# One attention and mixer block on one core: narrow matmuls gathered in two of a group's six slots

## The chip, the core and the metric

The kernel runs on one core of one Trainium2 chip. The core has five engines with a queue of instructions each: PE (TensorE, matmuls), DVE (VectorE), ACT (ScalarE), POOL (GpSimd) and SP (here it issues the DMAs). The metric is the device time of one execution in microseconds; lower is better.

## The reference

Three stages follow one another on inputs of 2 batches, 8 heads, 768 positions and head size 64 (a model width of 512):

```
q_assign = argmax(q_n @ c_n)          # 16 centroids per head
k_assign = argmax(k_n @ c_n)
mask = q_assign[:, None] == k_assign[None, :]
scores = where(mask, scale * q @ k.T, -1e9)
attn = exp(scores - max) / sum        # rows
x = attn @ v                          # -> [2, 768, 512]
...
theta = x @ w_theta
y = w_tok_r @ (x * cos(theta)) + w_tok_i @ (x * sin(theta))
u = x + y;  x = u + relu(u @ w_ch)
...
u = x + V.T @ (U.T @ x)
out = u + relu(u @ w_ch1) @ w_ch2
```

The change touches the first stage alone, the masked attention.

## The kernel before

A *group* is one batch with two of its heads; there are eight (NG = 8, the loop variable `g`). A head's 768 positions are six tiles of 128. The function `attention` runs the groups one after the other, and each group is written out as six *slots* `p` = 0 to 5. The order of the code is the order of every engine's queue; nothing reorders it later. One slot holds

- `scores_pair(g, h, a)`: the scores of two key tiles of one head (8 matmuls, tile `st`, line 303; wide, with 128 rows of output), which ACT turns into exponentials (tile `p`, line 308, four instructions on three banks);
- `max_pair(g + 1, ...)`: scores of the next group for its row maxima (4 matmuls, tile `smax`, line 251; wide), which DVE reduces from three banks (tile `mx`, line 255); after slots 2 and 5 `max_join` puts a head's maxima together (lines 260, 270, 271).

Besides there are the *narrow* matmuls, which write 32 rows of output or fewer:

- `pv`, the value products (line 316): twelve steps a group, taken from the queue `pvq` by `next_pv`; the code puts up to four into each of slots 1, 3 and 5. After the last, ACT copies the result to `xT` (line 323);
- `sum_keys`, the row sums of one half of the keys (tile `l`, line 335), which DVE transposes (tile `lt`, line 338); `row_sums` then takes the reciprocals (lines 343, 345);
- `max_rows`, the maxima as rows (tile `mrow`, line 281), copied by ACT;
- `sims`, the similarities with the centroids (line 121), the first of the items of `assign_items(g)`. DVE transposes them (tile `s_t`, line 124), and the items after it (lines 128 to 152, DVE) make the one-hot assignments that `mask_rows` needs.

Work without a fixed place stands in the queue `bg`: splitting q and k of group g + 2 and packing them by DMA, the assignments, `spread` and `norm_x` (lines 357 and 361, DVE). `fill(t)` takes items off it until their listed costs come to `t`; when `bg` is empty it takes steps of the conversion of the later weights (lines 388, 392 and 396 on DVE, one weight tile in three steps; 384 and 401 on ACT, 405 on POOL). Each slot ends with `fill(1.8)`.

PSUM has eight banks, handed out in turn: `bank()` takes the first of the list `ring` and puts it at the end again. From the first `pv` step of a group to its last, two of them are kept out of the ring. A slot takes three banks for `st` and three for `smax`.

`prologue` prepares groups 0 and 1 and also runs all items of `assign_items(2)`, ahead of `mask_direct(1, 0)` of slot 0 (line 181), whose result the first `smax` matmul of that slot needs. After the attention, `mixer` does the other two stages.

Of the kernel before, what the change touches and what calls it, by code (L numbers as in the profile page):

```python
# [24 lines left out]
NG = B * NP  # L25
# [16 lines left out]
def tile_cluster_block(ctx: ExitStack, tc: tile.TileContext, qk, v, cent, wth, wr, wi, wch,  # L42
# [24 lines left out]
    def give(keep):  # L67
        ring.extend(kept.pop(keep))
# [43 lines left out]
    def cols(hf):  # L112
        return slice(hf * HALF, (hf + 1) * HALF)
# [214 lines left out]
    def sum_keys(g, a):  # L328

        ps = bank("l")  # L330
        for kt in range(3 * a, 3 * a + 3):
            for h in range(2):
                for hf in range(2):
                    o = 32 * (2 * h + hf)
                    nc.tensor.matmul(out=ps[o:o + 32, :HALF], lhsT=ones, rhs=pt[g, h, kt][:, cols(hf)],  # L335
                                     start=(kt == 3 * a), stop=(kt == 3 * a + 2))
        lt = slot("lt")[:, :HALF]
        nc.vector.transpose(lt, ps[:, :HALF])
        lsum[g, a] = lt
# [330 lines left out]


    bg = deque()

    owed = [0.]

    def fill(t):

        owed[0] += t
        while owed[0] > 0:
            if bg:  # L680
                c, f = bg.popleft()
                f()
                owed[0] -= c
            else:
                conv_step()
                owed[0] -= 1.
# [7 lines left out]
    def attention():  # L694


        ORDER = [(0, 0), (0, 2), (0, 4), (1, 0), (1, 2), (1, 4)]
        pvq = deque()
        held[0] = True

        def next_pv():
            g, kt, hf = pvq.popleft()
            pv(g, kt, hf)
            if kt == NT - 1 and hf:
                pv_out(g)

        for g in range(NG):
            nxt = g + 1 < NG
            if nxt:
                load_v(g + 1)  # L710
            if g + 2 < NG:
                bg.extend(split_items(g + 2, nc.gpsimd))
                if g > 0:
                    bg.extend(assign_items(g + 2))
            if g + 3 < NG:
                for i in range(2):
                    load_raw(g + 3, i)
            if g == 1:
                conv_load.extend(weigh_in(wth, NP * DM, wth_t))
                conv_start()  # L720
            if g == 2:
                tok = [c for p in zip(weigh_in(wr, NT * S, wr_t), weigh_in(wi, NT * S, wi_t)) for c in p]
                conv_load.extend(tok[:6])
                conv_start()
                late = tok[6:]
            if g == 6:
                conv_load.extend(late)
                conv_start()
            if not nxt:
                for t in range(NP):  # L730
                    bg.append((0, lambda t=t: split_x(0, t, nc.gpsimd)))
            order = [(1, 0), None, (1, 2), None, (1, 4), None] if g == 0 else ORDER
            for p in range(NT):
                ready = len(pvq)
                if order[p]:
                    h, a = order[p]
                    scores_pair(g, h, a)
                    if h:
                        pvq.extend((g, kt, hf) for kt in (a, a + 1) for hf in range(2))
                if g == 0 and p < 2:  # L740
                    mask_direct(1, p, nc.scalar if p else nc.vector)
                if nxt:
                    max_pair(g + 1, p // 3, 2 * p % 6)
                    if p % 3 == 2:
                        max_join(g + 1, p // 3)

                while conv_after:
                    conv_after.popleft()()
                if p == 3 and g + 2 < NG:
                    mask_rows(g + 2)  # L750
                if g > 0 and p == 1:
                    sum_keys(g - 1, 1)
                if p == 5:
                    sum_keys(g, 0)
                if p % 2:
                    for _ in range(min(ready, 4)):
                        next_pv()
                if g > 0 and p == 1:
                    row_sums(g - 1)
                if g > 0 and p == 5:  # L760
                    bg.appendleft((.95, lambda: norm_x(g - 1)))
                    bg.appendleft((.97, lambda: spread(g - 1)))
                fill(1.8 if nxt else 2.)
                if g > 0 and p == 1:
                    max_rows(g, 1)
                if nxt and p == 3:
                    max_rows(g + 1, 0)
            while bg:
                fill(.5)
        held[0] = False  # L770
        while len(pvq) > 1:
            next_pv()
        nc.scalar.activation(out=warm, in_=warm, func=AF.Sin)
        next_pv()
        sum_keys(NG - 1, 1)

    def prologue():
        hot = slot("hot", BF16)
        nc.vector.memset(hot[:, :512], 0.0)
        hp = bank("hot", "hot")  # L780

        def heat(n):

            for _ in range(n):
                nc.tensor.matmul(out=hp, lhsT=hot[:, :P], rhs=hot[:, :512], start=True, stop=True)

        nc.sync.dma_start(out=cst_sb, in_=cst)
        nc.sync.dma_start(out=cent_sb, in_=cent)
        for g in range(2):
            for i in range(2):  # L790
                load_raw(g, i)
        nc.vector.memset(warm, 1.0)
        nc.scalar.activation(out=warm, in_=warm, func=AF.Sqrt)
        nc.vector.memset(ones, 1.0)
        nc.vector.memset(cblk, 0.0)
        for j in range(2):
            nc.vector.memset(kmul[64 * j:64 * j + 64, 0:1], BIG if j else 1.0)
            nc.vector.memset(kmul[64 * j:64 * j + 64, 1:2], -BIG if j else 0.0)
        nc.vector.memset(kmul[:, 2:3], -BIG)
        nc.vector.memset(halfpi, TWO_PI / 4)  # L800
        init_packs(0, nc.gpsimd)
        heat(9)

        nc.vector.tensor_tensor(csq, cent_sb, cent_sb, op=ALU.mult)
        nc.vector.tensor_reduce(cn2[:, 0:1], csq, axis=AX.X, op=ALU.add)
        nc.scalar.activation(out=cn2[:, 1:2], in_=cn2[:, 0:1], func=AF.Sqrt)
        nc.scalar.activation(out=warm, in_=warm, func=AF.Exp)
        nc.vector.tensor_scalar_add(cn2[:, 1:2], cn2[:, 1:2], 1e-6)
        nc.vector.reciprocal(cn2[:, 2:3], cn2[:, 1:2])
        for j in range(2):  # L810
            nc.vector.tensor_scalar(cdup[:, j], cent_sb, cn2[:, 2:3], None, op0=ALU.mult)
        nc.vector.tensor_copy(cvals, cst_sb[:, 128:160])
        nc.vector.tensor_copy(identb, ident)
        ct = bank("ct")
        nc.tensor.transpose(ct[:, :P], cdup.rearrange("p a d -> p (a d)"), ident)
        cv = ct[:, :P].rearrange("p (a h c) -> p a h c", a=NP, h=2)
        nc.vector.tensor_copy(cblk[0:64, :, 0:16], cv[0:64, :, 0])
        nc.vector.tensor_copy(cblk[64:128, :, 16:32], cv[64:128, :, 1])

        def run(items):  # L820
            for it in items:
                it[1]()

        its, its1 = assign_items(0), assign_items(1)
        for i in range(2):
            split_hi(0, i)
        split_lo(0, 0, nc.gpsimd)
        run(its[:1])
        pack_direct(0, 0)
        pack_direct(0, 1)  # L830
        pack(0, main=())
        load_v(0)
        for i in range(2):
            load_raw(2, i)

        init_packs(1, nc.gpsimd)
        heat(14)
        run(its[1:])
        run(its1[:1])
        mask_direct(0, 0, nc.vector)  # L840
        mask_direct(0, 1, nc.scalar)
        split_lo(0, 1, nc.gpsimd)
        pack_low(0, (0, 1))
        for i in range(2):
            split_hi(1, i)
            split_lo(1, i, nc.gpsimd)
        pack_direct(1, 0)
        pack(1, main=(1,))
        pack_low(1, (0,))
        for a in (0, 2, 4):  # L850
            max_pair(0, 0, a)
        max_join(0, 0, act=True)
        max_pair(0, 1, 0)
        max_pair(0, 1, 2)
        max_rows(0, 0)
        init_packs(2, nc.gpsimd)
        scores_pair(0, 0, 0)
        max_pair(0, 1, 4)
        max_join(0, 1)
        run(its1[1:])  # L860
        scores_pair(0, 0, 2)
        heat(2)
        scores_pair(0, 0, 4)
        heat(2)
        max_rows(0, 1)
        run(assign_items(2))
        give("hot")

    def mixer():
# [136 lines left out]
```

## Time and profile before

| | us |
|---|---|
| three runs, median (lowest to highest) | 702.51 (698.29 to 702.58) |
| the profiled execution, its own time | 700.68 |
| its span, first to last instruction | 698.9 |
| PE busy in the span | 684.9 |
| DVE busy in the span | 456.6 |
| ACT busy in the span | 303.3 |

The span is what the trace covers; the 1.8 us between it and the execution's own time lie around the program. The attention runs from about 31 us to about 240 us of the span. PE's busy share counts pipelined matmuls whose ends are modelled, so how fast it goes is read from the starts of successive rows.

### The profile page before, as it was taken

What the parts mean: (1) busy time and instruction counts of PE and PEld (TensorE: products, weight loads), DVE (VectorE), ACT (ScalarE), POOL (GpSimd) and SP (SyncE); (2) the same over time, 40 slices, a digit from 0 to 9 for tenths busy, and PEclk for the clock granted to TensorE, in tenths of its full rate; (3) what the DMA queues carried; (4) which work ended last, traced back from release to release, by engine and by line L of the source; (5) the groups of instructions that cost most, each with busy time, mean ns of one, the idle gap of its engine ahead of it and who ended that gap; (6) DMA issues with size and microseconds to landing.
All of it is one profiled execution on the core that took longest, in us unless ns stands there. A gap on an engine that the chain in (4) does not pass through costs nothing.

```text
span 698.9 us, 11387 instructions
## 1 busy us (share of the span) xinstructions
PE 684.9 (98%) x4492; PEld 545.7 (78%) x4492; DVE 456.6 (65%) x752; ACT 303.3 (43%) x617; POOL 186.3 (27%) x186
## 2 busy tenths in 40 slices
PE   7799999999999999999999999999999999999997
PEld 3456566565565599999999998888888889888986
DVE  6967987987989476568684985565555656432222
ACT  8636566665677555554555442322222222211110
POOL 9413323323238432114244120222121212100000
PEclk9899999999999999999999999999999999999999
DMA  6779667766322211013220220112122120000112
GB/s 213 189 158 295 199 157 191 218 162 137 126 91 90 92 40 38 1 31 106 80 66 3 90 91 1 46 46 90 51 86 77 59 76 30 1 1 0 61 47 74
DMA packets 21109, 63.11 MB, mean 90 GB/s; under 512 B 4192, under 2 KB 6112, under 8 KB 21056
## 3 DMA queue, kind: packets, MB, share of 16 engines
q1 hardware_dynamic: 21056, 62.39, 30.1%
q8 instruction: 35, 0.57, 0.3%
q14 instruction: 18, 0.15, 0.1%
HBM read 40.94 MB, written 3.15 MB: 63 GB/s over the span
## 4 chain that ended last, share of the span: by engine, by line
PE 89%; DVE 6%; ACT 2%; issue 1%; DMA 1%; POOL 1%; SPq 0%; DVEq 0%; POOLq 0%
PE g L634 19%; PE acc L654 19%; PE y L520 14%; PE st L303 8%; PE pv L316 8%; PE h L538 5%; PE th L478 5%; PE l L335 4%; PE smax L251 4%; DVE mx L255 2%; PE h L589 2%; DVE cv L396 1%; PE th L482 1%; PE sims L121 1%; DMA raw<-in_qk_dram 1%
## 5 line engine op out<-in xcount | busy, mean ns | idle before, releaser
L405 POOL TENSOR_TENSOR wl<-cv,wh 128x768 fp32r<-128x768 f32 (+1 forms) x40 | 78.3, 1959 | 232.6 <-ACT wh L401 175.3
L641 DVE SCALAR_TENSOR_TENSOR gl<-g,gh 128x512 fp32r<-128x512 f32 x48 | 33.1, 690 | 133.1 <-ACT gh L639 133.1
L639 ACT ACTIVATE gh<-g 128x512 fp32r<-128x512 f32 x48 | 28.7, 599 | 206.2 <-PE g L634 206.2
L255 DVE TENSOR_REDUCE mx<-smax 128x1 f32<-128x512 f32 x144 | 90.0, 683 | 24.3 <-PE smax L251 24.0
L308 ACT ACTIVATE p<-st 128x512 f32<-128x512 f32 x192 | 79.2, 506 | 26.6 <-PE st L303 26.1
L520 PE MATMUL y<-wh,z 128*128 128x384 f32 x384 | 87.6, 340 | 0.3 <-ACT z L498 0.3
L634 PE MATMUL g<-uh,wh 128*128 128x512 f32 (+1 forms) x256 | 86.9, 340 | 0.0
L634 PE MATMUL g<-uh,wl 128*128 128x512 f32 (+1 forms) x256 | 86.5, 338 | 0.0
L634 PE MATMUL g<-ul,wh 128*128 128x512 f32 (+1 forms) x256 | 86.1, 336 | 0.0
L303 PE MATMUL st<-qp,kp 128*128 128x256 f32 (+1 forms) x384 | 79.9, 351 | 0.8 <-ACT qp L284 0.3
L654 PE MATMUL acc<-gh,wh 128*128 128x512 f32 x192 | 75.9, 395 | 0.0
L654 PE MATMUL acc<-gh,wl 128*128 128x512 f32 x192 | 75.6, 394 | 0.0
L654 PE MATMUL acc<-gl,wh 128*128 128x512 f32 x192 | 75.3, 392 | 0.0
L303 PEld LDWEIGHTS st<-qp,kp 128*128 128x128 f32 x384 | 57.2, 191 | 18.2 <-issue 6.0
L520 PEld LDWEIGHTS y<-wh,z 128*128 128x128 f32 x384 | 66.9, 188 | 0.5 <-ACT z L498 0.5
L316 PE MATMUL pv<-p,v 128*32 128x384 f32 x768 | 66.2, 487 | 0.0
L392 DVE SCALAR_TENSOR_TENSOR cv<-st,cv 128x768 int32<-128x768 int32 (+2 forms) x42 | 64.6, 1537 | 1.0
L634 PEld LDWEIGHTS g<-ul,wh 128*128 128x128 f32 x256 | 48.5, 189 | 6.1
L634 PEld LDWEIGHTS g<-uh,wl 128*128 128x128 f32 x256 | 48.5, 189 | 5.8
L634 PEld LDWEIGHTS g<-uh,wh 128*128 128x128 f32 x256 | 48.4, 189 | 5.7
L316 PEld LDWEIGHTS pv<-p,v 128*32 128x32 f32 x768 | 24.1, 110 | 36.0 <-issue 35.4
L520 PE MATMUL y<-wl,z 128*128 128x384 f32 x192 | 48.8, 335 | 0.0
(128 smaller groups left out, 1172.9 us busy)
## 6 DMA issues: line engine op xcount, KB each, us to landing
st<-in_w_dram SPq DMA_DIRECT2D x20, 768.0 KB, 4.0
raw<-in_qk_dram SPq DMA_DIRECT2D x16, 384.0 KB, 4.9
qp<-hi SPq DMA_DIRECT2D x26, 192.0 KB, 2.9
st<-in_wr_dram SPq DMA_DIRECT2D x6, 768.0 KB, 4.3
st<-in_wi_dram SPq DMA_DIRECT2D x6, 768.0 KB, 4.2
kp<-hi SPq DMA_DIRECT2D x32, 96.0 KB, 3.0
qp<-lo SPq DMA_DIRECT2D x32, 96.0 KB, 2.8
v<-in_v_dram SPq DMA_DIRECT2D x8, 384.0 KB, 4.0
```

Source lines behind the costliest of these rows:

```text
L255: nc.vector.tensor_reduce(mx_t[g, h][:, o:o + n], ps.rearrange("p (n w) -> p n w", n=n), axis=AX.X, op=ALU.max)
L303: nc.tensor.matmul(out=ps[:, c:c + n], lhsT=kp[s, h, w][:, (a + j) * P:(a + j + 1) * P], rhs=qp[s, h, w][:, q0:q0 + n], start=(w == 0), st ...
L308: nc.scalar.activation(out=pt[g, h, a + j][:, q0:q0 + n], in_=ps[:, c:c + n], func=AF.Exp, scale=float(D) ** -0.5)
L316: nc.tensor.matmul(out=pvt[g][hf][r:r + 32, :HALF], lhsT=v_t[g][:, kt, r:r + 32], rhs=pt[g, r // 64, kt][:, cols(hf)], start=(kt == 0), st ...
L392: nc.vector.scalar_tensor_tensor(t, self.hw, SIGN, t, op0=ALU.bitwise_and, op1=ALU.bitwise_or)
L405: nc.gpsimd.tensor_tensor(t[:, :c.w], c.t, f32(c.hi[:, :c.w]), op=ALU.subtract)
L478: nc.tensor.matmul(out=ps[:, 1], lhsT=xs[b, t][a][:, st * P:(st + 1) * P], rhs=wv[c], start=(n == 0), stop=(n == 11))
L520: nc.tensor.matmul(out=yps[u, j][hf][:, :HALF], lhsT=lhs, rhs=w[st][e][:, hf * HALF:(hf + 1) * HALF], start=(st == 0 and n == 0), stop=(st ...
L538: nc.tensor.matmul(out=ps[hf][:, :HALF], lhsT=wv[a], rhs=xs[b, t][c][:, hf * HALF:(hf + 1) * HALF], start=(n == 0), stop=(n == 11))
L634: nc.tensor.matmul(out=ps[:, o:o + w], lhsT=wv[a], rhs=us[b, t][e][:, s0:s0 + w], start=(n == 0), stop=(n == 11))
L641: nc.vector.scalar_tensor_tensor(gl, ps, 0.0, f32(gh), op0=ALU.max, op1=ALU.subtract)
L654: nc.tensor.matmul(out=aps[c, e], lhsT=wv[a], rhs=g[x], start=(first and i == 0), stop=(last and i == 2))
```

## The change

The slots 2 and 5 (`BURST`) now hold all narrow matmuls: rows of maxima, row sums, up to six value-product steps, and in slot 5 also the similarities of group g + 3, one group earlier than before. `fill` gets 4.8 in those two slots and 0.3 in the four others (10.8 a group, as before). The other items of `assign_items(g + 3)` are kept in `assign` and go into `bg` at the start of the next group. In the prologue the last four items of group 2 are kept back in the same way.

```diff
+    assign = {}
...
+        BURST = (2, 5)
...
-                if g > 0:
-                    bg.extend(assign_items(g + 2))
+                bg.extend(assign.pop(g + 2))
...
-                if g > 0 and p == 1:
-                    sum_keys(g - 1, 1)
-                if p == 5:
-                    sum_keys(g, 0)
-                if p % 2:
-                    for _ in range(min(ready, 4)):
+                if p in BURST:
+                    if p == 2 and g > 0:
+                        max_rows(g, 1)
+                        sum_keys(g - 1, 1)
+                    if p == 5:
+                        if nxt:
+                            max_rows(g + 1, 0)
+                        sum_keys(g, 0)
+                    for _ in range(min(ready, 6)):
                         next_pv()
-                if g > 0 and p == 1:
+                    if p == 5 and g + 3 < NG:
+                        (_, sims), *assign[g + 3] = assign_items(g + 3)
+                        sims()
+                if g > 0 and p == 2:
                     row_sums(g - 1)
...
-                fill(1.8 if nxt else 2.)
-                if g > 0 and p == 1:
-                    max_rows(g, 1)
-                if nxt and p == 3:
-                    max_rows(g + 1, 0)
+                fill(2. if not nxt else 4.8 if p in BURST else .3)
...
-        run(assign_items(2))
+        its2 = assign_items(2)
+        run(its2[:4])
+        assign[2] = its2[4:]
```

On PE, at the border from group 1 to group 2, the similarities (`sims`) stood between the row maxima and the scores of slots 0 and 1. Before:

```order
L251 MATMUL smax<-kp_87,qp_85 128x256 x2
L251 MATMUL smax<-kp_87,qp_85 128x512
L121 MATMUL sims<-raw_0_732,cblk 32x384
L121 MATMUL sims<-raw_1_734,cblk 32x384
L121 MATMUL sims<-raw_0_732,cblk 32x384
L121 MATMUL sims<-raw_1_734,cblk 32x384
L303 MATMUL st<-qp_101,kp_103 128x512
L303 MATMUL st<-qp_102,kp_104 128x512
```

Now they stand at the end of slot 5 of group 1, behind the value products:

```order
L316 MATMUL pv<-p_792,v_461 32x384 x2
L316 MATMUL pv<-p_946,v_461 32x384 x2
L121 MATMUL sims<-raw_0_728,cblk 32x384
L121 MATMUL sims<-raw_1_730,cblk 32x384
L121 MATMUL sims<-raw_0_728,cblk 32x384
L121 MATMUL sims<-raw_1_730,cblk 32x384
L303 MATMUL st<-qp_101,kp_103 128x512
L303 MATMUL st<-qp_102,kp_104 128x512
```

They moved from the inside of a wide stretch to the last place of a narrow one.

On DVE, at the same border (from the transpose of the row sums in slot 5 to the reductions of `smax` in slot 0), before:

```order
L338 STREAM_TRANSPOSE lt<-l 128x384
L357 STREAM_TRANSPOSE rb<-rl 128x768
L361 TENSOR_TENSOR xT_727<-xT_727,rb 128x768
L255 TENSOR_REDUCE mx_1084<-smax 128x1
L255 TENSOR_REDUCE mx_1084<-smax 128x2
L255 TENSOR_REDUCE mx_1084<-smax 128x1
L124 STREAM_TRANSPOSE s_t<-sims 128x384
L128 TENSOR_REDUCE mxc<-s_t 128x24
```

Now:

```order
L338 STREAM_TRANSPOSE lt<-l 128x384
L124 STREAM_TRANSPOSE s_t<-sims 128x384
L357 STREAM_TRANSPOSE rb<-rl 128x768
L361 TENSOR_TENSOR xT_883<-xT_883,rb 128x768
L392 SCALAR_TENSOR_TENSOR cv<-st,cv 128x768
L396 SCALAR_TENSOR_TENSOR cv<-st,cv 128x768
L388 TENSOR_SCALAR cv<-cv 128x768
L255 TENSOR_REDUCE mx_1095<-smax 128x1
L255 TENSOR_REDUCE mx_1095<-smax 128x2
```

The transpose of the similarities moved ahead of `spread` and `norm_x`, and three conversion steps now stand ahead of the reductions of slot 0.

On DVE, at the end of the prologue, before:

```order
L128 TENSOR_REDUCE mxc<-s_t 128x24
L132 TENSOR_TENSOR eqw<-s_t,mxc 128x384
L138 TENSOR_TENSOR eqw<-eqw,cvals 128x384
L143 TENSOR_REDUCE mi<-eqw 128x24
L147 TENSOR_TENSOR eqw<-eqw,mi 128x384
L152 STREAM_TRANSPOSE eqw<-eqw 128x384
L181 TENSOR_SCALAR kp_95<-oht 16x384 x2
L255 TENSOR_REDUCE mx_501<-smax 128x1
```

Now:

```order
L128 TENSOR_REDUCE mxc<-s_t 128x24
L132 TENSOR_TENSOR eqw<-s_t,mxc 128x384
L181 TENSOR_SCALAR kp_95<-oht 16x384 x2
L255 TENSOR_REDUCE mx_496<-smax 128x1
L255 TENSOR_REDUCE mx_496<-smax 128x2
L255 TENSOR_REDUCE mx_496<-smax 128x1
L138 TENSOR_TENSOR eqw<-eqw,cvals 128x384
```

Four instructions moved from ahead of line 181 to behind the first reductions.

## Rows read from the trace of the kernel before

**Rows 1.** Busy time by stretch: PE, PEld, DVE, ACT, POOL, then granted clock.

```profile
35.00:36.00 1.00, 0.90 (x3) 0.84 (x4) 0.10 (x1) 0.00 (x0) 1.00 (x2) 0.50 0.98 221
...
135.00:160.00 25.00, 25.00 (x226) 15.02 (x224) 20.91 (x41) 14.56 (x33) 7.28 (x11) 1.00 0.60 150
```

**Rows 2.** Timeline of PE, groups 2 and 3: start, duration, what, count.

```profile
101.95 2.76 PE L316 MATMUL pv<-p,v 128*32 128x384 f32 x32
104.65 1.66 PE L303 MATMUL st<-qp,kp 128*128 128x512 f32 x8
...
110.00 2.14 PE L335 MATMUL l<-p,ones 128*32 128x384 f32 x24
111.96 2.76 PE L316 MATMUL pv<-p,v 128*32 128x384 f32 x32
114.54 0.34 PE L281 MATMUL mrow<-identb,m 128*2 128x128 bf16 x6
114.82 1.66 PE L303 MATMUL st<-qp,kp 128*128 128x512 f32 x8
116.32 0.85 PE L251 MATMUL smax<-kp,qp 128*128 128x512 f32 x4
117.01 1.56 PE L303 MATMUL st<-qp,kp 128*128 128x512 f32 x8
118.41 0.86 PE L251 MATMUL smax<-kp,qp 128*128 128x512 f32 x4
119.20 2.79 PE L316 MATMUL pv<-p,v 128*32 128x384 f32 x32
```

**Rows 3.** Timeline of PE at the start of group 0.

```profile
31.21 0.82 PE L174 MATMUL oht<-eqw,identb 128*16 128x384 bf16 x4
35.10 1.62 PE L251 MATMUL smax<-kp,qp 128*128 128x512 f32 x4 [3.07 <-ACT hi L188]
36.65 1.45 PE L174 MATMUL oht<-eqw,identb 128*16 128x384 bf16 x4
```

**Rows 4.** Timeline of DVE at the start of group 0.

```profile
31.66 0.36 DVE L138 TENSOR_TENSOR eqw<-eqw,cvals 128x384 bf16<-128x384 bf16 x1
...
33.84 1.04 DVE L181 TENSOR_SCALAR kp<-oht 16x384 fp32r<-16x384 f32 x2
```

**Rows 5.** Timeline of PE: two places in groups 1 and 5 where it waits.

```profile
68.56 0.34 PE L281 MATMUL mrow<-identb,m 128*2 128x128 bf16 x6 [1.10 <-DVE m L271]
...
177.50 2.11 PE L303 MATMUL st<-qp,kp 128*128 128x512 f32 x8
```

**Rows 6.** Timeline of DVE in groups 3 and 4; in brackets the idle time ahead.

```profile
112.21 0.58 DVE L338 STREAM_TRANSPOSE lt<-l 128x384 f32<-128x384 f32 x1 [0.68 <-PE l L335]
...
113.19 0.50 DVE L132 TENSOR_TENSOR eqw<-s_t,mxc 128x384 bf16<-128x384 f32 x1
...
131.23 0.94 DVE L357 STREAM_TRANSPOSE rb<-rl 128x768 f32<-128x768 f32 x1
132.27 0.96 DVE L361 TENSOR_TENSOR xT<-xT,rb 128x768 f32<-128x768 f32 x1
133.14 1.88 DVE L255 TENSOR_REDUCE mx<-smax 128x1 f32<-128x512 f32 x3
...
149.35 0.96 DVE L396 SCALAR_TENSOR_TENSOR cv<-st,cv 128x768 int32<-128x768 int32 x1
...
152.29 0.55 DVE L388 TENSOR_SCALAR cv<-cv 128x768 int32<-128x768 int32 x1
152.88 0.96 DVE L392 SCALAR_TENSOR_TENSOR cv<-st,cv 128x768 int32<-128x768 int32 x1
```

**Rows 7.** Timeline of ACT in group 3.

```profile
124.00 1.64 ACT L308 ACTIVATE p<-st 128x512 f32<-128x512 f32 x4
125.50 0.93 ACT L384 ACTIVATE cv<-st 128x768 f32<-128x768 f32 x1
...
127.75 0.92 ACT L401 ACTIVATE wh<-cv 128x768 fp32r<-128x768 f32 x1
```

## The prediction

> **What bounds the kernel now.** I read the busy time by stretch first. In a stretch of the attention PE has no idle time in 25 us and runs at the full granted clock, 1.00 (2.4 GHz); DVE is busy 20.91 of the 25, ACT 14.56 [rows 1]. So PE sets the pace, and DVE is near enough to set it wherever its work falls in the wrong order. Then I read PE's timeline by the starts of successive rows, to see what PE pays besides its matmuls [rows 2]. Eight `st` matmuls that follow narrow ones take 1.50 us until the next row starts (114.82 to 116.32); the same eight after wide ones take 1.40 (117.01 to 118.41). Four `smax` take 0.69 when wide ones follow (116.32 to 117.01) and 0.79 when narrow ones do (118.41 to 119.20). And 32 `pv` records (four steps) take 2.58 when other narrow ones follow (111.96 to 114.54) and 2.69 ahead of wide ones (101.95 to 104.65). One trip from wide to narrow and back thus costs 0.10 + 0.10 + 0.11 = 0.31 us. Last I read the places where PE does wait [rows 3, 5] and DVE's timeline next to them [rows 4, 6].
>
> **Trips saved.** In PE's order the attention with its prologue goes from narrow to wide 35 times before and 22 times now: the steady groups have two bursts where they had four (rows of sums and products, products and maxima, sums and products, similarities). 13 x 0.31 = 4.0 us gained, on PE's own path. The ends are 13 x 0.20 = 2.6, if the 0.11 of the third comparison belongs to `mrow`, and 4.4 if the first product after a wide row also saves (2.61 against 2.58, 119.20 and 111.96 with what follows).
>
> **The prologue.** PE waits 3.07 us ahead of its first `smax` of slot 0 [rows 3]. The row names an ACT copy; by the timelines it is line 181 on DVE, which starts at 33.84 and takes 1.04 (to 34.88), behind four items of the assignment of group 2, from 31.66 on [rows 4]. These items move behind the reductions of slot 0. Line 181 can then start when its input is there, 31.21 + 0.82 = 32.03, say 32.1: 1.7 us earlier, and PE with it. After the wait of 3.07 PE runs at a granted clock of 0.50 (1.2 GHz) [rows 1]: its `smax` took 1.62 where others take 0.85, and `oht` 1.45 where the one ahead took 0.82 [rows 2, 3], 1.4 us in all. With a wait of some 1.4 instead I take it that the clock stays, since the wait of 1.10 in group 1 left the row behind it at its usual 0.34 [rows 2, 5]. Gain 3.1; ends 0 (POOL or the packs are late instead) and 3.1. The four items cost nothing at their new place: in group 0 DVE has no conversion to do.
>
> **Waits that go.** `max_rows` stood one slot behind the maxima it needs and waited 1.10 for DVE in group 1; now it comes two slots or more behind them. In group 5 eight `st` took 2.11 where the usual is 1.56 [rows 2, 5], behind a `fill` in a slot without narrow matmuls; such slots get 0.3 now. Together 1.65; ends 0 and 3.
>
> **What the order on DVE costs.** The similarities end each burst of slot 5, and their transpose stands on DVE ahead of `spread`, `norm_x` and three conversion steps, and these stand ahead of the reductions of slot 0. DVE takes its instructions in order. The row says so: it idled 0.68 us for the row sums, while `eqw` at 113.19, whose input had long been there, stood behind and did not start [rows 6]. The Trainium skill (page "TensorE: Matmul & The Clock Gate", section "Architectural detail: the array is 16× 32×32, not 1× 128×128") has the rule, that VectorE's queue is strictly in order; it speaks against this change, and the trace agrees. If DVE could pass the transpose, this term would be nought and the sum 693.0.
>
> So from the end of the row sums DVE stands through six product steps (6 x 2.58 / 4 = 3.87 us) and the similarities. Let S be the start of the first `st` after the burst. The transpose of a narrow result starts 0.25 after PE's next row (111.96 and 112.21) [rows 2, 6]. Then, by starts: transpose 0.60, `spread` 1.04 (131.23 to 132.27), `norm_x` 0.87 (to 133.14), conversions 0.96 + 0.96 + 0.55. DVE comes to slot 0's reductions at S + 5.2. PE meanwhile does slot 0 and the `st` of slot 1 and wants its `smax` at S + 3.6 (114.82 to 118.41 is just that stretch). There it stops: with two banks held for `pv` six are left in the ring, a slot takes six, so slot 1's three `smax` banks are those of slot 0. The first comes free after one reduction of 0.68, at S + 5.9, the third two further steps of 0.6 later, at S + 7.1; the last matmul there takes 0.23. Slot 1 ends at S + 7.35 instead of S + 4.29 (118.41 to 119.20 less the trip's 0.10): 3.06 us late. After that the banks of slot 2 are free in time, since DVE's next three reductions end at S + 8.8 and PE wants the last bank at S + 9.2. The delay isn't given back: nothing else on PE was waiting. It falls at four borders (group 1 to 2 up to group 4 to 5; in group 0 there is no conversion yet, and from group 5 on no similarities). At one of them the three steps are of a 512-wide tile, two thirds of 2.47, so 2.24 late. 3 x 3.06 + 2.24 = 11.4 us lost. The ends are 0 (nothing surfaces) and 13.5, with DVE's 5.2 a tenth longer at each border.
>
> Slot 2's burst is different: its DVE work (row sums, assignment, one or two conversions) starts when the sums end, four products' time before the burst does, and is through about when the first `smax` of slot 3 is.
>
> **ACT in three wide slots.** Three batches of exponentials take 3 x 1.50 (124.00 to 125.50) in some 6.3 us of wide matmuls. In groups 2 and 4 a magnitude (0.93) and a copy of the weights (0.92) [rows 7] now stand ahead of the second batch, with no narrow matmuls to hide them; the bank of slot 4 that slot 5 wants then comes about 0.5 late. 2 x 0.5 = 1.0 lost; ends 0 and 9 (1.85 in five groups).
>
> SP's order hardly moves: raw data for the early similarities are asked for at the start of the group and needed at its end. POOL has the same work. The mixer behind is not touched.
>
> **Sum.** 700.7 (the profiled execution) - 4.0 - 3.1 - 1.65 + 11.4 + 1.0 = 704.4 us. The median of the three runs is 702.5, and they spread over 4.3 us, so the profiled one is as good a base. A change of 1%, 7 us, is about what a measurement of this kernel can tell from none.
>
> **Rivals.**
> (a) *The wait on DVE does not reach PE.* For it: DVE is busy for 20.91 of 25 us now, and PE does not idle [rows 1]. Against: there its `fill` comes in portions of 1.8 with a narrow burst behind each pair; here 3 us of conversions and divisions stand in one piece ahead of the reductions. Without the 11.4 the time is 693.0, faster by 1.1%. Chance 0.11.
> (b) *PE's clock falls in the new waits.* The place is slot 1 after each of the four borders, where PE stands for 2.3 us and then starts one matmul group per reduction. A wait of 3.07 was followed by a granted clock of 0.50 from 35 us on [rows 1, 3]; the wait of 1.10 was not. The new one lies between. If it falls, the stretch behind costs what it cost there, 1.4 us, four times: 704.4 + 5.6 = 710.0, slower by 1.3%. It decides if a wait of some 2.3 us counts as the long one did. [...] Chance 0.15.
> (c) *ACT becomes the bound of the wide slots*, in all groups rather than two: 1.85 us less what the banks absorb, say 1.3, in five groups: 704.4 + 5.5 = 710. For it: three wide slots without relief; against: ACT is busy 14.56 of 25. Chance 0.12.
> (d) *Trips cost less than the starts say*, or the narrow work merely takes on the price: 4.0 falls to 2.6 or below, 706 to 708. This lies in the forecast's range.
>
> **How the numbers follow.** The forecast, 704.4, has 0.62 with a range of its own from 699 to 709 (the ends of the trips, the prologue and ACT). Of that 0.58 is within 1% and 0.04 slower. With (a) nearly all faster, (b) nearly all slower and half of (c) slower: faster 0.10, within 1% 0.67, slower 0.23. For 8 in 10 the range reaches part of the way to (a) and to (b): 696 to 711.
>
> **What would show it.** Right: in the changed profile PE has about 13 fewer narrow stretches; DVE idles about 4 us ahead of line 124 in slot 5 of groups 0 to 4, named to PE `sims`; the `smax` of slot 1 of groups 2 to 5 starts some 2 us after the `st` ahead of it ends, named to DVE; the wait of 3.07 at 35 us is cut to about 1.4. Wrong: groups 2 to 5 take no longer from border to border than before; the waits stand at `st` and name ACT, (c); or the granted clock shows 0.50 in the attention, (b).

## The result, and the profile after

| | us | ratio to before |
|---|---|---|
| before, median of 4 runs (lowest to highest) | 700.4 (698.28 to 702.58) | |
| changed, median of 4 runs | 710.21 (709.2 to 712.28) | 1.0131, interval 1.0105 to 1.0156 |
| changed, the profiled execution (its span) | 709.2 (707.4) | |

The change costs 9.8 us, 1.3%, and the interval is clear of no change. The forecast was 704.4, no change within 1%. The time lies inside the stated range, 696 to 711, at its upper edge, but outside 699 to 709, the range of the sum by itself: what holds it is the part that was added for the rivals.

The waits of PE, added up by what they waited for (us in total, times, longest):

```profile
PE smax L251 <- DVE mx L255: 7.3, 5, 1.9
PE mrow L281 <- ACT p L308: 2.1, 1, 2.1
```

Both lines are new. PE's timeline shows where they stand: the start of group 0, where 1.20 us is left of the long wait in the prologue [rows 3]; slot 1 of group 2; group 3 from its border on; slot 1 of groups 4 and 5; then groups 6 and 7.

```profile
34.17 0.94 PE L251 MATMUL smax<-kp,qp 128*128 128x512 f32 x4 [1.20 <-ACT qp L177]
...
81.60 1.70 PE L251 MATMUL smax<-kp,qp 128*128 128x512 f32 x4 [1.76 <-DVE mx L255]
...
104.57 1.68 PE L303 MATMUL st<-qp,kp 128*128 128x512 f32 x8
106.09 0.86 PE L251 MATMUL smax<-kp,qp 128*128 128x512 f32 x4
106.79 1.57 PE L303 MATMUL st<-qp,kp 128*128 128x512 f32 x8
109.64 1.70 PE L251 MATMUL smax<-kp,qp 128*128 128x512 f32 x4 [1.29 <-DVE mx L255]
111.18 2.38 PE L303 MATMUL st<-qp,kp 128*128 128x512 f32 x8
113.35 1.48 PE L251 MATMUL smax<-kp,qp 128*128 128x512 f32 x4
...
139.75 1.70 PE L251 MATMUL smax<-kp,qp 128*128 128x512 f32 x4 [1.83 <-DVE mx L255]
141.29 1.56 PE L303 MATMUL st<-qp,kp 128*128 128x512 f32 x8
...
168.44 1.99 PE L251 MATMUL smax<-kp,qp 128*128 128x512 f32 x4 [1.87 <-DVE mx L255]
...
212.03 0.49 PE L251 MATMUL smax<-kp,qp 128*128 128x512 f32 x1 [0.59 <-DVE mx L255]
...
225.76 0.34 PE L281 MATMUL mrow<-identb,m 128*2 128x128 bf16 x6 [2.14 <-ACT p L308]
```

Read the starts. From the border at 104.57 the `st` of slot 2 should follow after 4.29 us, the time that the prediction worked out for two slots without a wait; it starts 6.61 after it, at 111.18, so 2.32 late. The idle in brackets is only part of that: the four `smax` behind it take 1.54 from start to next start instead of 0.70, since each waits for one more reduction. The same sum at the other three borders gives 2.78, 2.86 and 3.15; 11.1 us in all. DVE's timeline at the same border says why:

```profile
104.69 0.58 DVE L124 STREAM_TRANSPOSE s_t<-sims 128x384 f32<-128x384 f32 x1 [3.92 <-PE sims L121]
105.20 0.94 DVE L357 STREAM_TRANSPOSE rb<-rl 128x768 f32<-128x768 f32 x1
106.24 0.96 DVE L361 TENSOR_TENSOR xT<-xT,rb 128x768 f32<-128x768 f32 x1
107.12 0.42 DVE L388 TENSOR_SCALAR cv<-cv 128x512 int32<-128x512 int32 x1
107.57 0.69 DVE L392 SCALAR_TENSOR_TENSOR cv<-st,cv 128x512 int32<-128x512 int32 x1
108.30 0.69 DVE L396 SCALAR_TENSOR_TENSOR cv<-st,cv 128x512 int32<-128x512 int32 x1
108.91 3.67 DVE L255 TENSOR_REDUCE mx<-smax 128x1 f32<-128x512 f32 x6
```

It stands 3.92 us for the similarities, then does the divisions and three conversion steps, and only at 108.91 the reductions of slot 0, whose `smax` ended about 107. In the profile before, the same reductions followed `norm_x` at once [rows 6].

The clock is the part that the forecast left out of its sum. Stretches behind that wait (busy time of PE, PEld, DVE, ACT, POOL, then the granted clock):

```profile
110.00:112.00 2.00, 1.80 (x8) 1.32 (x8) 2.00 (x5) 2.00 (x6) 1.06 (x1) 0.91 0.97 267
112.00:114.00 2.00, 2.00 (x9) 1.71 (x8) 1.03 (x2) 2.00 (x5) 1.96 (x2) 0.50 0.97 389
```

0.50 is 1.2 GHz. `st` took 2.38 there and `smax` 1.48; 30 us later, behind an idle time that reads longer (1.83), `st` took its usual 1.56. At the border to group 5 the clock fell as in group 3, at the border to group 2 it did not. From the start of `st` in slot 2 to `mrow` it is 3.59 us in group 3 and 3.48 in group 5 against 2.17 in group 2: 2.7 us for the two. A trace shows one execution, and the clock is not the same in all of them: the mean granted clock of an execution of the kernel before lies between 0.999 (698.25 us) and 0.990 (703.23 us), the slower ones mostly at the lower clock. So "two of four borders" is what this execution shows.

The wait in group 7 belongs to ACT:

```profile
219.93 1.64 ACT L308 ACTIVATE p<-st 128x512 f32<-128x512 f32 x4 [4.18 <-PE st L303]
221.43 0.87 ACT L401 ACTIVATE wh<-cv 128x768 fp32r<-128x768 f32 x1
222.16 3.06 ACT L463 ACTIVATE xh<-xT 128x768 fp32r<-128x768 f32 x4
225.09 1.65 ACT L308 ACTIVATE p<-st 128x512 f32<-128x512 f32 x4
```

In the last group there are no `smax` matmuls: PE does 24 `st` in 4.45 us, three slots in a row, and needs twelve exponentials for their banks. Four copies for the mixer (`xh`, line 463) and one of the weights, 3.93 us together, stand between the first four and the second. In group 6 it is DVE that waits for ACT, at a conversion step ahead of reductions; behind these PE waits 0.59 and 0.26:

```profile
206.35 0.56 DVE L388 TENSOR_SCALAR cv<-cv 128x768 int32<-128x768 int32 x1 [1.69 <-ACT cv L384]
```

### The profile page after: what moved, and what is told of

It is laid out like the page before. It is cut to its first block, busy times and chain, and to the rows that moved or that the text cites. A ratio compares the mean times of both kernels' runs of the same rounds, so it can differ in the third digit from the quotient of the medians.

```text
span 707.4 us, 11358 instructions
## 1 busy us (share of the span) xinstructions
PE 686.8 (97%) x4491; PEld 563.6 (80%) x4492; DVE 447.6 (63%) x752; ACT 303.1 (43%) x617; POOL 186.6 (26%) x186
## 3 DMA queue, kind: packets, MB, share of 16 engines
HBM read 40.94 MB, written 3.15 MB: 62 GB/s over the span
## 4 chain that ended last, share of the span: by engine, by line
PE 90%; DVE 5%; ACT 3%; issue 1%; DMA 0%; SPq 0%; DVEq 0%
PE g L634 19%; PE acc L654 19%; PE y L520 14%; PE pv L316 9%; PE st L303 8%; PE h L538 5%; PE l L335 5%; PE th L478 4%; PE smax L251 4%; DVE mx L255 2%; PE h L589 2%; PE th L482 1%; ACT p L308 1%; DVE cv L392 1%; DVE cv L396 1%
## 5 line engine op out<-in xcount | busy, mean ns | idle before, releaser
L405 POOL TENSOR_TENSOR wl<-cv,wh 128x768 fp32r<-128x768 f32 (+1 forms) x40 | 79.9, 1996 | 258.7 <-ACT wh L401 224.1
L303 PE MATMUL st<-qp,kp 128*128 128x256 f32 (+1 forms) x384 | 81.5, 357 | 0.4 <-ACT qp L284 0.2
L303 PEld LDWEIGHTS st<-qp,kp 128*128 128x128 f32 x384 | 60.1, 198 | 18.1 <-issue 7.2
L251 PE MATMUL smax<-kp,qp 128*128 128x512 f32 x192 | 47.1, 359 | 10.6 <-DVE mx L255 7.3
L316 PEld LDWEIGHTS pv<-p,v 128*32 128x32 f32 x768 | 35.4, 110 | 26.3 <-issue 14.2
```

Of the source, the lines that this page charges most:

```text
L251: nc.tensor.matmul(out=ps[:, c:c + w], lhsT=qp[s, h, 0][:, (a + j) * P:(a + j + 1) * P], rhs=kp[s, h, 0][:, k0:k0 + w], start=True, stop=True)
L303: nc.tensor.matmul(out=ps[:, c:c + n], lhsT=kp[s, h, w][:, (a + j) * P:(a + j + 1) * P], rhs=qp[s, h, w][:, q0:q0 + n], start=(w == 0), st ...
L316: nc.tensor.matmul(out=pvt[g][hf][r:r + 32, :HALF], lhsT=v_t[g][:, kt, r:r + 32], rhs=pt[g, r // 64, kt][:, cols(hf)], start=(kt == 0), st ...
L405: nc.gpsimd.tensor_tensor(t[:, :c.w], c.t, f32(c.hi[:, :c.w]), op=ALU.subtract)
```

## The experiments

**A. Only the order on DVE: the transpose of the similarities behind slot 5's `fill`.** The changed kernel; PE's order is the same.

```diff
+            def turn():
+                st["s"] = slot("s_t")[:, :HALF]
+                nc.vector.transpose(st["s"], ps[:, :HALF])
+
+            if late:
+                return turn
+            turn()
...
-                        sims()
+                        turn_s = sims(True)
...
                 fill(2. if not nxt else 4.8 if p in BURST else .3)
+                if p == 5 and g + 3 < NG:
+                    turn_s()
```

> The changed kernel with one thing moved on DVE alone: in slot 5 the transpose of the similarities stands behind that slot's fill instead of ahead of it; PE's order is the same. Theory A (DVE stands idle for the similarities and the fill then lies ahead of the reductions of slot 0, and the clock falls behind some of these waits): the waits of PE on DVE in slot 1 of groups 2 to 5 (11.1 us summed from the trace of the changed kernel) go, and with them the 2.8 us at half clock at two of them, so 709.2 - 13.9 = 695, about 0.993 of the kernel before. Rival B (three wide slots in a row cost PE this time by themselves, through ACT and the banks): the waits move to other rows, 703 or more, 1.004 or above.

Measured: 697.45 us, 0.9955 (0.994 to 0.9971), 12.8 us below the changed kernel's 710.21. The waits of slot 1 are gone at all four borders, and the granted clock is 1.00 throughout the groups. At the border to group 3:

```profile
103.87 1.68 PE L309 MATMUL st<-qp,kp 128*128 128x512 f32 x8
...
107.48 0.86 PE L257 MATMUL smax<-kp,qp 128*128 128x512 f32 x4
108.18 1.56 PE L309 MATMUL st<-qp,kp 128*128 128x512 f32 x8
```

The `st` of slot 2 follows 4.31 us behind the border. Nothing else was moved, so the 13.8 us of the borders and of the clock behind them hang on this one place in DVE's queue. Not all of it comes back: by the two traces, groups 2 to 5 together are 11.6 us shorter (116.29 and 104.72). In each of them the row sums of slot 2 now start 1.35 to 1.51 us after the last `smax`, where it was 0.90 in group 2 of the changed kernel: some 2.2 in all; the trace puts 0.21 of it in each group down to an exponential. This is what is missing from the expected 695. PE's waits in groups 6 and 7 (0.58, 0.26, 2.14, 0.21) are still there, but they stood in the 709.2 from which that was worked out.

**B. Only the order on PE: the similarities ahead of the value products in slot 5.** The changed kernel; DVE's order is the same.

```diff
-                    for _ in range(min(ready, 6)):
-                        next_pv()
                     if p == 5 and g + 3 < NG:
                         (_, sims), *assign[g + 3] = assign_items(g + 3)
                         sims()
+                    for _ in range(min(ready, 6)):
+                        next_pv()
```

> The changed kernel with the similarities ahead of the value products in the burst of slot 5 instead of behind them; DVE's order is the same as in the changed kernel. Theory A: the transpose then waits some 0.7 us and not 3.9, the fill runs beside the products, and the time is as in the run with the fill first, about 695 (0.993). If it is the early similarities themselves that cost (their bank, or the raw data), it stays at 705 or above.

Measured: 697.32 us, 0.9956 (0.9941 to 0.9972), the same as A. The transpose, where it stood, is harmless if its input comes before the products rather than after them. A and B name the pair that must not meet: matmuls at the end of a burst, and their first user ahead of other work in an in-order queue.

**C. The prologue's part alone**, on the kernel before.

```diff
+    kept2 = []
...
-                if g > 0:
-                    bg.extend(assign_items(g + 2))
+                bg.extend(assign_items(g + 2) if g > 0 else kept2)
...
-        run(assign_items(2))
+        its2 = assign_items(2)
+        run(its2[:4])
+        kept2.extend(its2[4:])
```

> The kernel before with only the prologue's part: the last four items of group 2's assignment are kept for group 0's queue. My sum: PE's first row maxima of group 0 start 1.7 us earlier, and with a short wait the clock stays at its full level, so 3.1 us less, 697.5 (0.9955). Rival: the start is earlier but POOL, the packs or the next wait take it back, no change (1.000).

Measured: 697.86 us, 0.9957 (0.9943 to 0.997), 3.4 us below the 701.22 of before in that comparison (3.0 by the ratio). The first `smax` waits 1.20 instead of 3.07 [rows 3], and it and the `oht` behind it run at the full clock:

```profile
32.24 0.94 PE L251 MATMUL smax<-kp,qp 128*128 128x512 f32 x4 [1.20 <-ACT qp L177]
33.11 0.82 PE L174 MATMUL oht<-eqw,identb 128*16 128x384 bf16 x4
```

From the start of the `oht` ahead to the first `pv` it is 4.53 us where it was 7.72 (31.21 to 38.93), 3.2 less. The wait of 1.10 in group 1 [rows 5] is 0.50 here. But what C gains is also all that A and B gain over before, although they save 13 trips as well.

**D. More trips: up to two product steps in each of the six slots**, on the kernel before; narrow to wide 52 times instead of 35.

```diff
-                if p % 2:
-                    for _ in range(min(ready, 4)):
-                        next_pv()
+                for _ in range(min(ready, 2)):
+                    next_pv()
```

> The kernel before with up to two value-product steps in each slot instead of four in every other one: the number of changes from narrow to wide on PE rises from 35 to 52. If a trip costs 0.31 us on PE's own path: 17 x 0.31 = 5.3 us more, 706 (1.0075). Rival, the trips are nearly free and what the starts show is only the modelled ends: no change (1.000 to 1.002), or a little faster through the evener load on DVE.

Measured: 704.13 us, 1.0049 (1.003 to 1.0068): 3.4 us by the ratio (2.9 by the medians) for 17 trips, 0.20 each (0.12 to 0.28), less than the expected 0.31. In a steady group, where nothing waits in either kernel, the price is the one read from the starts of rows. Two borders of this kernel, one group apart, and the second of the same borders before:

```profile
105.62 1.67 PE L303 MATMUL st<-qp,kp 128*128 128x512 f32 x8
...
132.71 1.67 PE L303 MATMUL st<-qp,kp 128*128 128x512 f32 x8
```

```profile
131.13 1.66 PE L303 MATMUL st<-qp,kp 128*128 128x512 f32 x8
```

27.09 us against 26.48 from 104.65 [rows 2] to 131.13 before, for two trips more: 0.30 each. The whole kernel shows less because some rows that ran late before, without a wait named, do not in D (0.28, 0.55, 0.36, 0.11 and 0.24 us in groups 4 to 6).

So the trips have their price, and saving them brought nothing in A and B. The mixer starts here in B, then in C:

```profile
235.94 0.39 PE L478 MATMUL th<-wh,xh 128*128 128x256 f32 x1
```

```profile
235.82 0.38 PE L478 MATMUL th<-wh,xh 128*128 128x256 f32 x1
```

Between the first `smax` of group 0 (33.28 and 32.24) and the mixer B takes 202.66 us and C 203.58, so B takes 0.92 less. In that stretch B waits 4.01 us at named places (four times 0.21 at the row sums, 0.58 and 0.26 in group 6, 2.12 and 0.21 in group 7) and C 0.88. Without the waits B would be 0.92 + 3.13 = 4.05 us shorter, 0.31 for each of 13 trips. That counts named waits alone: four `smax` rows of C also run 0.27 to 0.62 long (1.45 in all) without a wait named, and with those as waits it would be 0.20. In groups 2 to 5 by themselves B is 1.83 shorter, with 0.84 more of waits and 8 trips fewer, 0.33 each. On this reading the gain is there, and the waits eat it, 3.17 of the 4.01 in the last two groups. Three kernels tried to get these back.

**E. Group 7's ACT work into its two bursts.** B, with the copies `xh` queued in slot 2 and all of the group's conversion steps in slots 2 and 5.

```diff
-            if not nxt:
-                for t in range(NP):
-                    bg.append((0, lambda t=t: split_x(0, t, nc.gpsimd)))
...
-                fill(2. if not nxt else 4.8 if p in BURST else .3)
+                if not nxt and p == 2:
+                    for t in range(NP):
+                        bg.append((0, lambda t=t: split_x(0, t, nc.gpsimd)))
+                fill(4.8 if nxt and p in BURST else .3 if nxt else 6. if p in BURST else 0.)
```

> The kernel with the similarities ahead of the value products took 0.9956 of before, no less than the one with the prologue's part alone (0.9957). From the first smax to the mixer it was 0.92 us shorter; it had 13 trips fewer and 3.1 us more waits at named places. Theory: the trips are worth 4.0 us as predicted and the waits eat them, 2.3 of it in group 7, where four copies of ACT (split of x, 3.06 us) and the conversions stand between exponentials of three wide slots in a row. This kernel adds to that one only that group 7's copies and conversion steps stand in its two bursts. Expected: the waits of 2.12 and 0.21 in group 7 gone, 695.0 us, 0.9923 (0.991 to 0.9935). Rival: ACT is short of time in group 7 altogether, the wait comes back at another row of the group: 697.3, 0.9956.

Measured: 702.85 us, 1.0032 (1.0017 to 1.0047), 5.5 worse than B where 2.3 better was expected. PE's timeline in group 7:

```profile
222.90 0.73 PE L303 MATMUL st<-qp,kp 128*128 128x512 f32 x2 [1.66 <-ACT p L308]
...
229.18 1.12 PE L335 MATMUL l<-p,ones 128*32 128x384 f32 x2 [3.50 <-ACT p L308]
```

and DVE, ACT and POOL there:

```profile
222.82 2.48 DVE L392 SCALAR_TENSOR_TENSOR cv<-st,cv 128x768 int32<-128x768 int32 x1
225.33 2.44 DVE L396 SCALAR_TENSOR_TENSOR cv<-st,cv 128x768 int32<-128x768 int32 x1
...
227.80 0.84 ACT L401 ACTIVATE wh<-cv 128x768 fp32r<-128x768 f32 x1 [3.20 <-DVE cv L396]
228.55 3.14 ACT L308 ACTIVATE p<-st 128x512 f32<-128x512 f32 x8
...
218.73 8.23 POOL L465 TENSOR_TENSOR xl<-xT,xh 128x768 fp32r<-128x768 f32 x4 [0.58 <-PE st L303]
```

The wait of 2.12 went and two longer ones came. The copies feed POOL, which runs 8.23 us without a pause; beside it DVE's conversion steps take 2.48 and 2.44 instead of 0.96 [rows 6], as they did in the kernel before beside the same work of POOL (2.47 and 2.39); ACT stands 3.20 for them at its copy `wh`, and eight exponentials that were free to run stand behind that. The Trainium skill (page "SBUF — State Buffer", section "SBUF: two separate sides") says that VectorE and GpSimd share one pair of ports under an exclusive lock; these rows, 2.48 against 0.96, agree. After the wait of 3.50 the clock was 0.50 from 230 to 232.

**F. E, with three changes more**: two conversion steps fewer in slot 2 of group 6, two of slot 2's product steps ahead of the row sums, and 7 instead of 6 for `fill` in the bursts of group 7.

```diff
                         max_rows(g, 1)
+                        for _ in range(min(ready, 2)):
+                            next_pv()
+                            ready -= 1
                         sum_keys(g - 1, 1)
...
+                if nxt:
+                    fill(.3 if p not in BURST else 2.8 if g == 6 and p == 2 else 4.8)
+                else:
+                    fill(7. if p in BURST else 0.)
```

> As the kernel of the last group, and: in group 6 two conversion steps fewer in slot 2 (DVE stood 1.69 for a magnitude of ACT there, behind it the reductions that PE then waited 0.58 + 0.26 for), and in slot 2 of a group two of the six product steps between the rows of maxima and the row sums, so that the row sums find a free bank (they waited 0.21 for an exponential in four groups). Theory: all of these waits go, 2.3 + 0.84 + 0.84 = 4.0 us less than the kernel with the similarities first: 693.3, 0.9899 (0.9885 to 0.992). Rival: the trips' gain is smaller than 0.31 and only group 7's wait comes off: 695 (0.9923), or the row sums come late for DVE and nothing more is gained.

Measured: 702.45 us, 1.0027 (1.0013 to 1.004). Group 6 lost its waits. Group 7 had those of E (1.69 and 3.90). In groups 2 to 5 the row sums no longer wait for an exponential, but `smax` waits for DVE at two new places (0.75 and 0.39), and the row sums once (0.26), so this was an exchange.

**G. The last group as it was before the change**, on B: narrow matmuls of group 7 in slots 1, 3 and 5 again, and F's smaller `fill` in group 6.

```diff
+                if not nxt:
+                    if p == 1:
+                        sum_keys(g - 1, 1)
+                    if p == 5:
+                        sum_keys(g, 0)
+                    if p % 2:
+                        for _ in range(min(ready, 4)):
+                            next_pv()
+                    if p == 1:
+                        row_sums(g - 1)
-                if p in BURST:
+                elif p in BURST:
...
-                fill(2. if not nxt else 4.8 if p in BURST else .3)
+                fill(2. if not nxt else .3 if p not in BURST else 2.8 if g == 6 and p == 2 else 4.8)
+                if not nxt and p == 1:
+                    max_rows(g, 1)
```

> The kernel with the similarities ahead of the value products (0.9956 of before), with the last group written as it was before the change (narrow matmuls in slots 1, 3 and 5, so one trip more) and, in slot 2 of group 6, two conversion steps fewer. Theory: the trips saved in the groups before are worth 0.31 us each and were eaten by the waits in groups 6 and 7: the waits of 0.58 + 0.26 in group 6 and of 2.12 + 0.21 in group 7 go, 0.3 for the trip and 0.4 for the wait that group 7 had before come back: 697.3 - 3.2 + 0.7 = 694.8, 0.9919 (0.9905 to 0.9935), below the kernel with the prologue's part alone (0.9957). Rival: the trips are worth less than that, or the waits come back elsewhere in these groups as they did when group 7's work was moved into its bursts: 697.3, 0.9956.

Measured: 694.77 us, 0.9913 (0.9893 to 0.9933), where 694.8 and 0.9919 were expected. It is below A and B and below C, the prologue's part alone: 3.1 us below C by the medians, for 12 trips fewer. By the traces group 6 is 1.7 and group 7 1.4 us shorter than in B. Group 7 in PE's timeline:

```profile
204.88 3.06 PE L303 MATMUL st<-qp,kp 128*128 128x512 f32 x16
207.86 2.14 PE L335 MATMUL l<-p,ones 128*32 128x384 f32 x24
...
212.68 1.91 PE L303 MATMUL st<-qp,kp 128*128 128x512 f32 x9
214.90 1.44 PE L303 MATMUL st<-qp,kp 128*128 128x512 f32 x7 [0.31 <-ACT qp L284]
```

16 `st` at a time leave ACT the row sums and products to catch up in, and 0.31 is the only wait of the group.

**H. Work for PE in the wait.** The changed kernel; in slot 1 of groups 2 to 5 the last third of the scores is computed three more times into the same bank, with the same values.

```diff
+            if part is THIRDS[2]:
+                for j, q0, n in part * again:
+                    for w in range(2):
+                        nc.tensor.matmul(out=ps[:, :n], lhsT=kp[s, h, w][:, (a + j) * P:(a + j + 1) * P],
+                                         rhs=qp[s, h, w][:, q0:q0 + n], start=(w == 0), stop=(w == 1))
...
-                    scores_pair(g, h, a)
+                    scores_pair(g, h, a, 3 if p == 1 and 2 <= g <= 5 else 0)
```

> The changed kernel, but in slot 1 of groups 2 to 5 PE computes the last third of the scores three more times (six more 512-wide matmuls, about 1.05 us, the same values into the same bank), while it waits for DVE's reductions. Theory: the wait for DVE stays as long as it was, but PE is at work for most of it and its clock is not cut; the 2.7 us that the half clock took in groups 3 and 5 come back: 707.5 us, 1.009 of before, with a granted clock of 1.00 at all four borders. Rival: the 8 st and 4 smax behind the wait were slow for another reason (ACT's exponentials late behind its own wait for DVE), then 710, 1.013. If the matmuls added to the path: 714, 1.019.

Measured: 708.27 us, 1.0109 (1.0086 to 1.0132); the interval overlaps that of the changed kernel, so the 1.9 us between the two medians are not settled by the times. The trace is plainer. PE's timeline in group 3 and one row of group 7, then a stretch of group 3:

```profile
108.33 1.54 PE L309 MATMUL st<-qp,kp 128*128 128x512 f32 x6
109.79 1.69 PE L251 MATMUL smax<-kp,qp 128*128 128x512 f32 x4
111.32 1.57 PE L303 MATMUL st<-qp,kp 128*128 128x512 f32 x8
...
223.96 3.54 PE L340 MATMUL l<-p,ones 128*32 128x384 f32 x24 [0.21 <-ACT p L313]
```

```profile
112.00:114.00 2.00, 1.92 (x20) 1.35 (x22) 2.00 (x5) 2.00 (x6) 1.81 (x2) 1.00 0.99 399
```

Line 309 is the repeated work, six matmuls at each of four places. `smax` starts 5.08 us after the border with it (104.71) and 5.07 without, so it costs nothing; the clock stays at 1.00 at all four borders and `st` takes 1.57 where it took 2.38. Groups 3 and 5 are 1.2 and 1.3 us shorter than in the changed kernel, and groups 2 and 4 as long. The wait is DVE's, and the slow matmuls behind it were PE's clock. What the time does not show of this went in group 7: there the edit changes nothing, but the clock fell to 0.51 behind the wait of 2.12, the 24 matmuls of `l` took 3.54 us instead of 2.14, and the group is 1.7 longer. As the clock falls in one execution and not in another, that the added work kept it up is likely from two borders of two, but not proved.

**I. Two conversion steps fewer behind the transpose**: the changed kernel with 2.8 in slot 5, and 0.5 more in each slot without narrow matmuls.

```diff
-                fill(2. if not nxt else 4.8 if p in BURST else .3)
+                fill(2. if not nxt else 4.8 if p == 2 else 2.8 if p == 5 else .8)
```

> The changed kernel with fill 2.8 instead of 4.8 in slot 5, and 0.8 instead of 0.3 in the four slots without narrow matmuls: the transpose of the similarities stands where it stood, spread and norm_x behind it, but one conversion step there instead of three. Theory: two steps of 0.96 us come from between the transpose and the reductions, PE is late by 0.9 to 1.1 at each of four borders instead of 2.8, and the wait is too short for the clock to fall: 710.2 - 7 - 2.7 = 700.5, 0.999 (0.997 to 1.002). Rival: it is DVE's standing for the similarities as such that costs, whatever stands behind it: 708 or more, 1.01. If the steps count but the clock still falls at two borders: 703, 1.0025.

Measured: 704.45 us, 1.0049 (1.0029 to 1.007): 5.8 below the changed kernel, where 9.7 was expected. PE is late by 0.92, 1.60, 1.33 and 0.93 (4.8 instead of 11.1), at a clock of 1.00: two of the borders are as expected, two above the 0.9 to 1.1, the second with a new wait of 0.38 for ACT in it. At that border DVE still stands 3.90 us for the similarities, so the standing by itself is not the price. From the border to group 2 to that of group 6 the trace is 8.3 us shorter. But groups 6 and 7 are 1.7 and 1.5 longer. In group 6 PE goes at the pace of DVE's reductions at two more places. In group 7 the wait for ACT is the same as in B, and this time the clock fell behind it. This kernel, then B:

```profile
219.78 0.41 PE L281 MATMUL mrow<-identb,m 128*2 128x128 bf16 x6 [2.12 <-ACT p L308]
```

```profile
220.00:222.00 2.00, 1.86 (x18) 0.60 (x16) 0.39 (x1) 2.00 (x6) 2.00 (x2) 0.50 0.00 0
```

```profile
213.29 0.34 PE L281 MATMUL mrow<-identb,m 128*2 128x128 bf16 x6 [2.12 <-ACT p L308]
```

```profile
214.00:216.00 2.00, 2.00 (x28) 0.78 (x24) 0.87 (x1) 2.00 (x6) 2.00 (x2) 1.00 0.04 8
```

## Why the prediction was wrong

| term of the sum | forecast | measured | from |
|---|---|---|---|
| trips | -4.0 | -4.0 (0.31 each) | B against C, named waits taken out; 0.30 in D's steady group, but 0.20 in D as a whole |
| prologue | -3.1 | -3.2 | C, by the starts of rows |
| waits that go | -1.65 | -1.1 | see below |
| order on DVE | +11.4 | +11.1 | four borders; A, B |
| clock at the borders | 0 (rival b: +5.6) | +2.7 | two of four borders in the one execution traced; H |
| ACT in wide slots | +1.0 | +2.0 | group 7, not 2 and 4 |
| DVE in group 6 | 0 | +0.85 | 0.59 + 0.26 |
| sum | +3.65 | +8.35 | |

The two traces differ by 8.5 us of span (707.4 and 698.9), the medians by 9.8 with an uncertainty of 1.8.

*Right.* What was named for the profile came: DVE idle for 3.92 ahead of line 124 (about 4 was said), the `smax` of slot 1 late and put down to DVE, the prologue's wait at 1.20 (about 1.4). The step that decided the sign, the order on DVE, was right in its place, its borders and its size; its one small error was the start of the reductions, 4.8 to 4.9 us behind S at the three borders with the long conversion steps, where 5.2 had been worked out. The prologue was right in size. The trips were right in the steady groups; that they come out at 4.0 in all is partly luck, since the comparison gives 2.6 to 4.0 by what is counted as a wait.

*Half right.* The wait of 1.10 in group 1 went with the change, 0.60 of it already with C. The longer `st` of group 5 [rows 5] is absent in C too, which has none of the bursts, and there a `smax` of group 6 runs 0.62 longer instead; so that 0.55 cannot be put down to the bursts.

*Wrong, the first step: the clock.* The sum took the new waits at the clock of 1.00 and kept the half clock as a rival that would strike at all four places or at none, with 0.15. It struck at two of four in the execution traced (0.50 from 112 to 114), at 1.4 and 1.3 us, the price that had been worked out for one. It was read from two waits, 3.07 with a fall and 1.10 without, and a new wait between them was counted as the shorter one. It should have stood in the sum as a term of its own, half of 5.6; then the forecast would have been 707.2.

*Wrong, the second step: the place of ACT's and DVE's shortage.* "Three batches of exponentials in some 6.3 us of wide matmuls" was applied to groups 2 and 4, where `smax` stands between the `st` and nothing surfaced. The same sentence holds far more strongly in group 7, which has no `smax`: three batches (4.5 us of ACT) and 3.9 us of copies in 4.45 us of matmuls. Before, each 16 `st` were followed by narrow work, and the group lost 0.3 there. The price was 2.35, less those 0.3. In group 6, which has only conversions left to fill its bursts with, DVE waited 1.69 us for a magnitude that stood behind other work of ACT, and PE 0.85 for DVE. Neither group was looked at as a stretch of its own; G, which changes only these two, shows what they took: 2.6 us from B by the medians, 3.2 by the traces.

*Rivals.* (a) fell with A and B. (b) came, at half of its places. (c) did not as it was stated: no group of the changed kernel that has `smax` waited for an exponential; with the borders mended (A, B) four of them did, for 0.21 each. (d) is not settled: D as a whole gives 0.20 a trip, which would make 2.6 of the 4.0, and its steady group 0.30.

*Open.* Why the clock fell behind some waits and not behind others of the same size isn't settled: no row ahead of the four borders tells them apart, and in group 7, which is the same code in the changed kernel, in B, in H and in I, it fell in H and I and not in the other two. And why G's row sums still wait 0.21 in four groups was not tried further, since F only exchanged that wait for others.

## What to carry to other kernels

When matmuls are moved to the end of a burst, look at what their first user stands ahead of in its own queue: the cost here was not the 3.9 us that DVE stood, but the reductions behind it that gave PE its banks, and either end could be moved to be rid of it. Gathering work saved its switches in the steady groups, but price the first and last passes of the loop by themselves: where the filler or the partner work has run out, the same grouping starves another engine. And give a wait that lies between one that cost the clock and one that did not a share of that cost in the sum, not only a rival's chance.

## What the runs showed of the chip that was not expected

- Waits that read 1.29 and 1.87 us were followed by a granted clock of 0.50, those of 1.76 and 1.83 were not; a wait of 2.12 in group 7 kept 1.00 in B and was followed by 0.50 in I and 0.51 in H. With six 512-wide matmuls in the middle of such a wait it was 1.00 at four places of four, at two of which it was 1.00 without them.
- A trip from 128-row to 32-row matmuls and back cost PE 0.30 us in a steady group with no wait on any other engine (D), and 0.20 (0.12 to 0.28) over the whole kernel.
- Beside four of POOL's subtractions in a row (8.23 us) DVE's two-input steps took 2.5 times as long (2.48 instead of 0.96), and ACT stood 3.20 for DVE.
